# Attention and a two-layer MoE block on one core: batch 0 masked by a bias matmul, one casting DMA queue for the weights and batch 1, four second-layer tiles at once, PSUM banks assigned by hand

## The chip, the cores and the metric

The kernel runs on one core of a Trainium2 chip. The metric is the device time of the core in microseconds (us). Before the change it was 321.75 us, the median of three runs (321.38 to 325.4).

The engines are named as in the profile: PE is TensorE (PEld its weight loads), DVE is VectorE, ACT is ScalarE, POOL is GpSimd, SP is SyncE. The profiler also records the clock that the chip grants TensorE; in these traces it is either full (1.00) or half (0.50).

## The reference, cut to what matters

```python
def _attn_ref(q, k, v):            # (8, 8, 576, 64), float32
    scores = scale * np.matmul(q, k.transpose(0, 1, 3, 2))
    mask_local = (rel >= 0) & (rel < 32)                       # heads 0 to 3
    mask_strided = (rel >= 0) & (pos_k % 32 == pos_q % 32)     # heads 4 to 7
    attn = softmax(np.where(masks, scores, -1e9))
    return np.matmul(attn, v)

def _moe_ref(x, w_in, w_out):      # x: 4608 tokens x 512, hidden size 2048
    r = np.maximum(x @ w_in, 0.0)
    return (r * r) @ w_out
```

A *unit* is one pair of heads of one batch. Each batch has four: units 4b and 4b+1 are local, 4b+2 and 4b+3 strided. A *chunk* is 512 of the 4,608 tokens, and there are nine. A chunk's first layer is 16 ReLUs of 128x512; its second layer is four output tiles with four groups of four matmuls each. Batch 0's attention has to be done before chunk 0 can be, and batch 1's before chunk 1.

## The kernel before

The kernel fills PE with MoE matmuls and puts the attention of later batches, step by step, between the groups of four matmuls. The steps of a unit are T (transposes of q and k), S (scores, exponentials, mask), D (probabilities times v, then the division by the row sum on DVE) and E (the transposition of the result for the MoE). For batch 0 there is nothing to fill with, and it has its own order. The matmuls write into eight banks of the memory PSUM: five for attention (`pt`), two for the first layer (`ph`), one for the second (`py`).

```python
    ps_h = ctx.enter_context(tc.tile_pool(name="ps_h", bufs=2, space=PS))
    ps_y = ctx.enter_context(tc.tile_pool(name="ps_y", bufs=1, space=PS))
    ps_t = ctx.enter_context(tc.tile_pool(name="ps_t", bufs=5, space=PS))
    ...
    def step_S(u):                       # scores of one unit into four banks, then
        ...
        expo(0, 0)                       # the exponentials on ACT, one a tick,
        later(1, lambda: expo(0, 1), u)  # and the masks as products on DVE
        later(2, lambda: (masks(0), expo(1, 0)), u)
        later(3, lambda: expo(1, 1), u)
        later(4, lambda: masks(1), u)
    ...
        # end of batch 0's order: n = sums, o = products with v, part = the first three
        # ReLU rows of chunk 0, unit by unit as its rows of x come
        order = [...
                 (due(d), 0), (n(c), 0), (o(c), 0), (lambda: part((a, b), (0,)), 0), (n(d), 0), (o(d), 0),
                 (lambda: part((a, b), (1, 2)), 0), (lambda: part((c,)), 0), (lambda: part((d,)), 0)]
    ...
    def loads(b):                        # a batch's loads and casts; for b == 1 also the w_out blocks
        ...
        w_out(0)
        if b < XB:
            load_qk_str(u + 2)
        cast_qk_local(u, pool2)
        w_out(1)
        cast_qk_local(u + 1, pool2)
        ...
        w_out(2)
        cast_v_local(u)
        cast_v_local(u + 1)
        w_out(3)
    ...
    for part in range(4):                # chunk 0's second layer: three output tiles at once,
        for j, pool in ((0, ps_h), (1, ps_h), (2, None)):
            add(0, 2, 4 * j + part, pool)
    for part in range(4):                # then the fourth
        add(0, 2, 12 + part, ps_h)
```

The softmax here doesn't subtract the row's maximum and nothing guards it: scores larger than these inputs give would overflow.

Of the kernel before, what the change touches and what calls it, by code (L numbers as in the profile page):

```python
# [14 lines left out]
def kernel(  # L15
# [30 lines left out]
    x_pool = ctx.enter_context(tc.tile_pool(name="x_pool", bufs=2))  # L46
    g_pool = ctx.enter_context(tc.tile_pool(name="g_pool", bufs=2))
# [6 lines left out]
    ps_h = ctx.enter_context(tc.tile_pool(name="ps_h", bufs=2, space=PS))  # L54
    ps_y = ctx.enter_context(tc.tile_pool(name="ps_y", bufs=1, space=PS))
    ps_t = ctx.enter_context(tc.tile_pool(name="ps_t", bufs=5, space=PS))
# [16 lines left out]
    ones = singles.tile([128, D], BF16)  # L73
    b0 = g_pool.tile([128, 16, 512], BF16, name="g_sb").rearrange("p a c -> p (a c)")
# [4 lines left out]

    ph_n = [0]  # L80

    def ph_tile():
        ph_n[0] += 1
        return ps_h.tile([128, 512], FP32, name="ph")

    nc.scalar.preload_act_table_set("natural_log_exp_and_others")
# [12 lines left out]
    def load_qk_local(u, eng, gate=None):  # L99
        b, p = units[u]  # L100
        s = st.setdefault(u, {})
        for name, src in (("q", q), ("k", k)):
# [7 lines left out]
            if gate is not None and name == "q":  # L110
                nc.gpsimd.tensor_copy(t[0:1, 0, 0:1], gate)
            eng.dma_start(out=t, in_=src[b, 2 * p:2 * p + 2]
                          .rearrange("h (p j) d -> p h (j d)", j=6))
            s[name + "f"] = t
# [71 lines left out]

    def load_v_str(u, eng):
        b, p = units[u]
        t = v_st.tile([SP_, 2, NJ * D], FP32, name="v_st")
        eng.dma_start(out=t, in_=v[b, 2 * p:2 * p + 2]  # L190
                      .rearrange("h (p j) d -> p h (j d)", j=NJ))
        st.setdefault(u, {})["vf"] = t
# [32 lines left out]
    def step_T(u, name):  # L225
# [5 lines left out]
        pt = ps_t.tile([128, S], BF16, name="pt")  # L231
# [13 lines left out]
        if name == "q" and u not in (1, 2, 3):  # L245
            nc.scalar.copy(o, i)
        else:
            nc.vector.tensor_copy(o, i)
# [5 lines left out]
    def step_S(u):  # L254
# [8 lines left out]
        banks = [[None, None], [None, None]]  # L263
        for half in range(2):
            for row in range(2):
                banks[row][half] = ps_t.tile([128, 512], FP32, name="pt")
            for i in range(hn):
                t = half * hn + i
                klo = w * t
                for row in range(2):  # L270
# [4 lines left out]
                    else:  # L275
                        lhsT, rhs = kT[rows, klo:klo + kn], qT[rows, w * t:w * (t + 1)]
                    nc.tensor.matmul(banks[row][half][0:kn, w * i:w * (i + 1)], lhsT, rhs,  # L277
                                     start=True, stop=True)

        def expo(row, half):  # L280
            lo = S * row + S // 2 * half
            nc.scalar.activation(e[0:kn, lo:lo + S // 2], banks[row][half][0:kn, 0:S // 2],  # L282
                                 AF.Exp, scale=scale)

        def masks(row):
# [3 lines left out]
            if u < 2:  # L289
                nc.vector.memset(x[0:32, 0], 0.0)  # L290

        expo(0, 0)
# [5 lines left out]
    def load_v_first():  # L298
        src = v[0, 0:4].rearrange("h (t p) d -> p (h t) d", p=QL)
        dst = b0[:, 0:n_l].rearrange("p (n d) -> p n d", d=D)  # L300
        nc.gpsimd.dma_start(out=dst[32:128], in_=src)
        nc.gpsimd.dma_start(out=dst[0:32, 1:4 * NL], in_=src[64:96, 0:4 * NL - 1])
        nc.gpsimd.dma_start(
            out=b0[0:SP_, n_l:n_l + n_s].rearrange("p (h c) -> p h c", h=4),
            in_=v[0, 4:8].rearrange("h (p j) d -> p h (j d)", j=NJ))

    def step_N(u):
        e, local = st[u]["e"], is_local(u)
        kn, hw = (128 if local else SP_), S // 2
        for half in range(2):  # L310
            pn = ph_tile() if u in first_order[0:2] else ps_t.tile([128, 512], FP32, name="pt")
# [7 lines left out]
    def step_O(u):  # L319
# [3 lines left out]
        for half in range(2):  # L323
            po = ps_t.tile([128, 512], FP32, name="pt")
# [17 lines left out]
    def step_D(u, part):  # L342
# [14 lines left out]
        po = ps_t.tile([128, 6, D + 1], FP32, name="pt")  # L357
# [3 lines left out]
        if part == 0:  # L361
            s["x"] = x_pool.tile([w, tot, D], BF16, name="x_l" if is_local(u) else "x_s")
# [11 lines left out]
    def step_E(u):  # L374
# [11 lines left out]
        px = ps_t.tile([128, S], BF16, name="pt")  # L386
# [17 lines left out]
    def mm1(c, ff, kks=range(4), order=range(4), pool=None):  # L404
# [3 lines left out]
        if kks[0] == order[0]:  # L408
            phs[ff] = ph_tile() if pool is None else pool.tile([128, 512], FP32, name="py")
# [13 lines left out]
    def mm2(c, i, pool=None):  # L423
        j, part = divmod(i, 4)
        g = gs[c]
        if part == 0:
            ys[c, j] = ps_y.tile([128, 512], FP32, name="py") if pool is None else ph_tile()
# [4 lines left out]
        if part == 3:  # L432
            y = y_pool.tile([128, 512], FP32, name="y")
            nc.scalar.copy(y, py)  # L434
            r0 = 512 * c + 128 * j
# [7 lines left out]
    def warm(n):  # L443
        if n:
            pw = ps_y.tile([128, 512], FP32, name="py")
# [257 lines left out]
```

## Time and profile before

| stage of the kernel before | from, to (us) | length | what limits it |
|---|---|---|---|
| batch 0's attention | 0 to 24.5 | 24.5 | hand-overs PE, ACT, DVE; half clock from 12.9 to 23.1 |
| first layer of chunk 0 | 24.5 to 37.3 | 12.8 | PE |
| second layer of chunk 0, batch 1's attention in it | 37.3 to 62.6 | 25.3 | PE, with 4.2 us of short waits |
| chunks 1 to 8 | 62.6 to 319.6 | 257.0 | PE |

The prediction below shows the page's PE and clock lines, the stage table, the waits and some of the second-layer stage. One more view is needed to read the result: PE in order of time at the end of batch 0. The columns are start and length in us, engine, line, operation with its tiles, how many, and in brackets how long PE stood idle just before and for whom.

```profile
21.07 0.63 PE L412 MATMUL ph<-xt,w_in_b 128*128 128x512 bf16 x1 [0.33 <-DVE xt L335]
21.64 0.69 PE L314 MATMUL pt<-e,ones 128*64 128x288 bf16 x4
22.12 0.69 PE L332 MATMUL pt<-e,g_sb 128*64 128x96 bf16 x12
22.74 0.78 PE L412 MATMUL ph<-xt,w_in_b 128*128 128x512 bf16 x2
...
24.49 0.59 PE L412 MATMUL ph<-xt,w_in_b 128*128 128x512 bf16 x2
```

L332 is the products with v, L412 the first layer's pieces. The last product (22.12) comes before nearly all pieces, so DVE can divide its rows while PE works through the pieces of the other units. The last piece follows at 24.49 with hardly a wait.

### The profile page before, as it was taken

Reading aid. Unit: us, or ns where it says so; the run is one execution under the profiler, and the core shown is the slowest. Engines: PE = TensorE matmul, PEld = TensorE weight load, DVE = VectorE, ACT = ScalarE, POOL = GpSimd, SP = SyncE. Lnnn points to the kernel's source line nnn. Section 1 sums busy time; section 2 is a strip of 40 time slices with the busy share of each in tenths; the row PEclk is TensorE's granted clock in tenths of the full one; section 3 lists DMA queues with packets and bytes.
Section 4 is the critical chain, followed back from the end, with each engine's and each line's share of the span. In section 5 each row is a group of like instructions: output and inputs, shape, how many; then the busy total and the mean of one; then the engine's idle time right before and its main releaser. Section 6 shows DMA issues by size and latency. Waiting matters only on the chain.

```text
span 319.6 us, 6138 instructions
## 1 busy us (share of the span) xinstructions
PE 300.0 (94%) x2322; PEld 149.5 (47%) x2364; DVE 170.7 (53%) x414; ACT 163.7 (51%) x337; POOL 87.8 (27%) x114
## 2 busy tenths in 40 slices
PE   7789978898999989999999999999999999999995
PEld 3454545444555444444444444444444444444442
DVE  6476463677956975676585557555555222222200
ACT  4576644477655755554554455545543443434311
POOL 8605472473930713271182015000000000000000
PEclk9859999999999999999999999999999999999999
DMA  7999999999999999999797677000411110000021
GB/s 182 172 205 227 221 155 251 186 328 208 198 162 210 197 212 182 212 242 188 183 211 167 145 159 133 35 33 33 53 51 36 55 42 36 33 33 35 35 96 66
DMA packets 87220, 44.79 MB, mean 140 GB/s; under 512 B 71768, under 2 KB 80376, under 8 KB 87000
## 3 DMA queue, kind: packets, MB, share of 16 engines
q1 hardware_dynamic: 77448, 34.81, 53.3%
q0 software_dynamic: 9744, 9.60, 18.9%
q8 instruction: 18, 0.29, 0.4%
q14 instruction: 10, 0.08, 0.1%
HBM read 36.89 MB, written 12.98 MB: 156 GB/s over the span
## 4 chain that ended last, share of the span: by engine, by line
PE 78%; DMA 9%; DVE 6%; ACT 3%; issue 2%; POOL 1%; SPq 0%; ACTq 0%; POOLq 0%
PE ph L412 33%; PE py L430 26%; PE ph L430 10%; PE pt L359 3%; PE pt L277 3%; DMA w_out_b<-in_moe_w_out_dram 3%; DMA q_st<-in_q_dram 3%; DMA kT_s<-in_k_dram 3%; DVE xt L396 1%; PE pt L388 1%; DVE e L288 1%; PE pt L233 1%; DVE g_sb L419 1%; ACT r L418 1%; ACT e L282 1%
## 5 line engine op out<-in xcount | busy, mean ns | idle before, releaser
L412 PE MATMUL ph<-xt,w_in_b 128*128 128x512 bf16 x557 | 143.3, 380 | 3.3 <-DVE xt L396 1.9
L418 ACT ACTIVATE r<-ph 128x512 bf16<-128x512 f32 x143 | 85.3, 597 | 99.5 <-PE ph L412 96.2
L419 DVE TENSOR_TENSOR g_sb<-r 128x512 bf16<-128x512 bf16 x144 | 71.2, 496 | 102.4 <-ACT r L418 101.9
L430 PE MATMUL py<-w_out_b,g_sb 128*128 128x512 bf16 x383 | 100.2, 379 | 1.3 <-issue 0.5
L430 PEld LDWEIGHTS <-g_sb 128*128 128x128 bf16 x576 | 52.9, 98 | 60.8 <-issue 4.3
L412 PEld LDWEIGHTS <-w_in_b 128*128 128x128 bf16 x576 | 51.7, 98 | 54.5 <-issue 1.3
L282 ACT ACTIVATE e<-pt 128x288 bf16<-128x288 f32 (+1 forms) x128 | 48.8, 406 | 17.0 <-PE pt L277 16.9
L430 PE MATMUL ph<-w_out_b,g_sb 128*128 128x512 bf16 x166 | 40.7, 379 | 1.9 <-DMA w_out_b<-in_moe_w_out_dram 1.2
L181 POOL CAST vl<-vl_st 128x768 bf16<-128x768 f32 x14 | 12.4, 886 | 60.2 <-DMA vl_st<-in_v_dram 58.1
L359 PEld LDWEIGHTS <-e 128*128 128x128 bf16 (+1 forms) x392 | 21.0, 97 | 15.6 <-DVE e L288 0.5
L371 DVE TENSOR_TENSOR x_s<-pt,rinv 72x384 bf16<-72x384 f32 (+1 forms) x42 | 21.4, 509 | 1.4
L288 DVE TENSOR_TENSOR e<-e,mask_str 72x576 bf16<-72x576 bf16 x32 | 18.0, 563 | 5.9 <-ACT e L282 5.6
L122 POOL CAST q_l<-q_st 96x768 bf16<-96x768 f32 x15 | 13.0, 865 | 21.9 <-DMA q_st<-in_q_dram 19.4
L288 DVE TENSOR_TENSOR e<-e,mask_loc 128x576 bf16<-128x576 bf16 x32 | 16.7, 523 | 1.7 <-ACT e L282 1.7
L122 POOL CAST k_l<-k_st 96x768 bf16<-96x768 f32 x15 | 13.3, 885 | 13.9 <-DMA k_st<-in_k_dram 13.8
L370 DVE RECIPROCAL rinv<-pt 96x6 f32<-96x6 f32 (+2 forms) x70 | 12.9, 184 | 7.8 <-PE pt L359 7.8
L434 ACT COPY y<-py 128x512 f32<-128x512 f32 x25 | 14.7, 587 | 4.0 <-PE py L430 4.0
L371 DVE TENSOR_TENSOR x_l<-pt,rinv 96x384 bf16<-96x384 f32 x28 | 15.5, 553 | 1.8 <-DMA xt<-x_l 0.9
L434 ACT COPY y<-ph 128x512 f32<-128x512 f32 x11 | 6.4, 586 | 19.4 <-PE ph L430 19.4
L197 POOL CAST vs<-v_st 72x1024 bf16<-72x1024 f32 x14 | 15.4, 1126 | 1.6 <-DMA v_st<-in_v_dram 1.3
L359 PE MATMUL pt<-vs,e 72*128 72x65 bf16 x224 | 13.7, 193 | 0.1
L182 POOL CAST vl<-vl_st 32x640 bf16<-32x640 f32 x14 | 11.9, 850 | 0.9
(77 smaller groups left out, 154.2 us busy)
## 6 DMA issues: line engine op xcount, KB each, us to landing
out_dram<-y SPq DMA_DIRECT2D x36, 256.0 KB, 2.0
vl_st<-in_v_dram SPq DMA_DIRECT2D x28, 144.0 KB, 4.0
v_st<-in_v_dram SPq DMA_DIRECT2D x14, 288.0 KB
q_st<-in_q_dram SPq DMA_DIRECT2D x8, 288.0 KB, 7.1
k_st<-in_k_dram SPq DMA_DIRECT2D x8, 288.0 KB, 7.9
q_st<-in_q_dram SPq DMA_DIRECT2D x16, 144.0 KB, 3.8
k_st<-in_k_dram SPq DMA_DIRECT2D x16, 144.0 KB, 5.9
w_in_b<-in_moe_w_in_dram POOLq DMA_DIRECT2D x4, 512.0 KB, 9.4
```

The costliest lines, as they stand in the source:

```text
L122: copy(t.rearrange("p j h d -> p h j d"), s[name + "f"].rearrange("p h (j d) -> p h j d", j=6))
L197: (copy or nc.gpsimd.tensor_copy)(t[:, :, 0:D], s["vf"].rearrange("p h (j d) -> p (h j) d", d=D))
L282: nc.scalar.activation(e[0:kn, lo:lo + S // 2], banks[row][half][0:kn, 0:S // 2], AF.Exp, scale=scale)
L288: nc.vector.tensor_tensor(x, x, m.to_broadcast([kn, n, w]), op=ALU.mult)
L359: nc.tensor.matmul(po[:, n - n0, :], e[0:kn, pos(n):pos(n) + 128], rhs[0:kn, src(n), 0:D + 1], start=True, stop=True)
L370: nc.vector.reciprocal(rinv[0:w, 0:m], po[0:w, 0:m, D:D + 1])
L371: nc.vector.tensor_tensor(x, po[0:w, 0:m, 0:D], rinv[0:w, 0:m].to_broadcast([w, m, D]), op=ALU.mult)
L412: nc.tensor.matmul(ph, w_in_b[:, kk, 128 * ff:128 * (ff + 1)], xt[kk][:, 512 * c:512 * (c + 1)], start=(kk == order[0]), stop=(kk == order ...
L418: nc.scalar.activation(r, ph, AF.Relu)
L419: later(1, lambda: nc.vector.tensor_tensor(g[:, ff, :], r, r, op=ALU.mult))
L430: nc.tensor.matmul(py, g[:, ff, 128 * j:128 * (j + 1)], w_out_b[:, ff, :], start=(ff == 0), stop=(ff == 15))
L434: nc.scalar.copy(y, py)
```

## The change

There are three intents. (1) Batch 0's masks leave DVE: a matmul writes minus 30,000 times the forbidden places into the PSUM bank first, and the scores accumulate on it. More dummy matmuls ("fillers") are to keep the clock full, and one load of batch 0's v moves from GpSimd's queue to ScalarE's, a third queue beside GpSimd's and SyncE's. (2) The w_out blocks and the q, k and strided v rows of batch 1 go through one casting queue on GpSimd in the order in which they are needed. (3) Chunk 0's second layer works on all four output tiles at once, the fourth in a bank taken from attention, and batch 1's steps are placed by hand at given groups, most of them in one lump at group 24. Banks are no longer taken from pools but from lists in strict rotation. The diff also has smaller edits that the cut below leaves out: batch 0's transposes go to the first layer's banks, its unit 1 is cast on DVE instead of GpSimd, and the loads of later batches are issued at other groups. The diff, cut to its core:

```diff
+    banks = {nm: [psum.tile([128, 512], FP32, name=f"{nm}{i}") for i in range(n)]
+             for nm, n in (("ph", 2), ("py", 1), ("pt", 5))}
+    def bank(nm):
+        t = banks[nm].pop(0)
+        banks[nm].append(t)
+        while id(t) in unread:
+            run_due(lambda x: x[1] == unread[id(t)])
+        return t
 ...
+                pss[row][half] = bank("pt")
+                if u < 4:
+                    bias = ...
+                    nc.tensor.matmul(pss[row][half][0:kn, 0:S // 2], ident[0:kn, 0:kn], bias,
+                                     start=True, stop=False, skip_group_check=True)
 ...
+        # (step, fillers after it)
+        order = [(t(0, "q"), 2), (t(0, "k"), 3), (S_(0), 2), (cast1("q"), 0), (t(2, "q"), 1), (t(2, "k"), 2),
+                 (cast1("k"), 0), (S_(2), 1), (n(0), 1), (t(3, "q"), 1), (t(3, "k"), 1), (S_(3), 1), (n(2), 1),
+                 (t(1, "q"), 1), (t(1, "k"), 1), (o(2), 1), (S_(1), 1), (n(3), 1), (o(0), 1), (n(1), 1),
+                 (lambda: part((a, b)), 0), (o(3), 0), (lambda: part((c,)), 0), (o(1), 0),
+                 (lambda: part((d,)), 0)]
 ...
+    def loads_1():
+        load_w_out(0)
+        load_qk_local_sw(4); load_qk_str(6)                      # (lines joined here)
+        load_w_out(1)
+        load_qk_local_sw(5); load_qk_str(7); load_v_str_sw(6); load_v_str_sw(7)
+        load_w_out(2); load_w_out(3)
+        ...                                                      # v of units 4, 5 on SyncE; the casts
 ...
     for part in range(4):
-        for j, pool in ((0, ps_h), (1, ps_h), (2, None)):
+        for j, pool in ((0, "ph"), (1, "ph"), (2, None), (3, "pt")):
             add(0, 2, 4 * j + part, pool)
-    for part in range(4):
-        add(0, 2, 12 + part, ps_h)
 ...
+    second(20, T_(6, "q"), T_(6, "k"), S_(6), T_(4, "q"), T_(4, "k"))
+    second(21, S_(4), T_(5, "q"))
+    second(22, T_(5, "k"))
+    second(23, S_(5))
+    second(24, *D_all(4), T_(7, "q"), T_(7, "k"), E_(4), S_(7), *D_all(5), E_(5), *D_all(6))
+    second(25, E_(6))
+    second(26, *D_all(7))
+    second(27, E_(7))
```

## The prediction

> **What bounds the kernel now.** I read the page first, then a table by stage, then who PE waited for in the one stage that the change rebuilds, then that stage in order of time.
>
> ```profile
> PE 300.0 (94%) x2322; PEld 149.5 (47%) x2364; DVE 170.7 (53%) x414; ACT 163.7 (51%) x337; POOL 87.8 (27%) x114
> ...
> PEclk9859999999999999999999999999999999999999
> ```
>
> PE is busy 94% of the 319.6 us span, so the bound is TensorE and a change can win only PE's idle time or its slow clock. The clock line says where: slices 2 and 3 (8 to 24 us) ran at 0.8 and 0.5 of full speed, the rest at 1. The stage table shows where PE idles (columns: length of the stretch, busy us of PE, PEld, DVE, ACT, POOL, then clock, DMA share, GB/s):
>
> ```profile
> 24.40:37.30 12.90, 12.59 (x68) 5.89 (x68) 7.39 (x16) 9.33 (x17) 6.80 (x10) 1.00 1.15 225
> 37.30:62.30 25.00, 20.83 (x248) 12.05 (x251) 14.27 (x34) 11.88 (x27) 13.38 (x18) 1.00 1.13 207
> ...
> 119.50:151.70 32.20, 31.67 (x253) 15.68 (x257) 20.41 (x47) 16.81 (x36) 12.94 (x16) 1.00 1.19 206
> ```
>
> The stages are batch 0's attention (0 to 24.4), first layer of chunk 0 (to 37.3), second layer of chunk 0 with batch 1's attention between its tiles (to 62.3), then the rest. From 119.5 on PE idles only 0.5 us per 32 us: nothing to win. The change touches the first 62 us. There the second-layer stage idles 25.00 - 20.83 = 4.2 us, which these waits make up:
>
> ```profile
> PE ph L430 <- DMA w_out_b<-in_moe_w_out_dram: 1.2, 1, 1.2
> PE pt L277 <- DVE kT L248: 1.1, 2, 0.6
> PE pt L388 <- DVE x_s L371: 0.8, 2, 0.5
> PE pt L277 <- ACT e L282: 0.5, 1, 0.5
> ```
>
> One late weight block costs 1.2 us; the rest are short waits for DVE and ACT inside attention, short because a group of second-layer matmuls stands between nearly every two attention steps:
>
> ```profile
> 54.20 0.81 PE L430 MATMUL ph<-w_out_b,g_sb 128*128 128x512 bf16 x3 [0.16 <-issue]
> 54.85 0.42 PE L388 MATMUL pt<-ident,x_l 96*128 96x96 bf16 x6
> 55.10 1.03 PE L430 MATMUL py<-w_out_b,g_sb 128*128 128x512 bf16 x4
> 55.97 0.53 PE L359 MATMUL pt<-vs,e 72*128 72x65 bf16 x12
> 56.34 1.03 PE L430 MATMUL ph<-w_out_b,g_sb 128*128 128x512 bf16 x4
> ```
>
> **What the Trainium skill says.** "TensorE: Matmul & The Clock Gate", section "What's actually happening": the array runs at half clock after an idle window of about 3.4 us and at full clock after a busy one. The trace agrees in kind: PE is busy in 5.83 of the 8 us from 8 to 16, and the clock record halves from 12.9 to 23.1 us (10.24 us, three such windows). "DMA: Bandwidth & Descriptors", section "Issuing engines are not separate DMA queues": all queues share the same 16 engines. The trace agrees: with q and k on SyncE's queue and w_out on GpSimd's, packets of 1,024 B that had run at 200 per us alone fall to about 100. "PSUM — Partial Sum Buffer", section "The four PSUM rules": a matmul with the start flag clears the accumulate bits of its whole bank, so the bias matmul must carry the flag and the score matmuls must not. That is how the change writes it; no run yet shows it.
>
> **Part 1: batch 0 masks as a bias (0 to 24.4 us).** Removed from DVE: eight mask products of 0.45 us and four memsets of 0.10, 4.0 us. Added on PE: 16 bias matmuls of 288 columns (512 columns take 0.216 us, so 0.12 each, 1.9 us) and 14 more filler matmuls (22 instead of 8, 3.0 us). ACT's work stays. DVE's products are partly in the chain, but ACT becomes the next bound: from the scores of the second unit on it has three units of exponentials (4 x 0.33) and four normalizers (0.71 + 0.68), 3 x 1.32 + 4 x 1.39 = 9.5 us. In the trace ACT works from 12.25 to 23.58 there, 11.3 us, so 1.8 us at most comes free. Against it stands the DMA: the first masked unit waits for its k rows until 10.86 us, and now one v tile (1,152 packets of 256 B; 743 such packets fell in the us from 57 on, so 1.55 us) is fetched at the same time on a third queue. I take 0.7 us of delay. Batch 0 ends about 1.1 us earlier: last piece of the first chunk at 23.4 instead of 24.5.
>
> **Part 2: one casting queue.** Counted from packets: a w block of 512 packets takes 2.56 us at 200 per us; q and k of a local unit about 1.5, of a strided unit 1.44, v of both strided units 1.44. w_in lands at 26.0 before and, with the duplicate v load gone, about 25.7 after. Adding down the new queue: w_out block 0 at 28.3, q and k of units 4 and 6 at 31, block 1 at 33.7, units 5 and 7 at 36.5, and with 3.1 us of v tiles between them block 2 at 43.4 and block 3 at 46. Before, the last block was issued at 44.84 and took at least 6.2 us to land: 51.1. So the weights come 5 us sooner and the wait of 1.2 us goes. GpSimd's casts of q and k now stand behind the issue of block 3, which waits for block 1: units 4's are ready about 36.8 rather than 28.7. That is why the new order begins batch 1 only after the first four second-layer groups, where before three transposes (0.26 each) were done in the first layer.
>
> **Part 3: four tiles at once, batch 1 in a lump.** First layer: 13 groups of 4 x 0.216 and the leftover pieces, 12.1 us, from 23.4 to 35.5. Four groups on block 0: 3.45 us, to 38.9. From here (t = 0) I went down the new instruction order of PE, ACT and DVE by hand, each instruction starting when the one before it on its engine and its operands and bank were done, with durations of the trace before: transpose 0.26, scores 0.36 to 0.40, second-layer group 0.86, ACT copy 0.64, exponential 0.33, DVE copy 0.46 (strided units) or 0.75 (local), mask 0.45, reciprocal and product 0.73 for a local half, 1.9 for a strided unit. The fourth output tile holds one of the five attention banks, so scores (four banks) and transposes wait for each other's readers. Results: unit 6's scores wait 0.66 for the k copy; unit 4's k transpose waits 1.5 for the third exponential of unit 6; its scores 0.44; unit 5's transposes and scores 1.1; then in the lump with no second-layer group in it, unit 4's output transpose waits 1.9 for DVE (0.73 + two masks + 0.73), unit 7's scores and unit 5's products 0.9, unit 5's output transpose 1.9, the last two transposes 0.9 each. Sum 10.2, with small ones 10.9 us. PE's own work in the stage is 12 groups (10.4) and 6.3 of attention. So batch 1 takes 23.3 us up to its last transpose, and five groups (4.3 us) come after it: t = 27.6, the second chunk starts at 66.5.
>
> **The sum.** Before, the second chunk effectively starts at 62.6 (62.3 with one wait for a copy). After: 66.5, +3.9 us. From there PE's order is the same in both kernels, and it is PE-bound: unchanged. Median before 321.75 + 3.9 = 325.7 by this walk.
>
> **Rivals.** (a) The walk is too strict: every idle us of PE in it is a hand-over between ACT, DVE and PE, and an error of 0.1 us in each of some thirty hand-overs is 3 us. Then only the weights' 1.2 us and batch 0's 1.1 count, and the time is 318 to 320. For it: the steps are placed by hand at particular groups, which looks like tuning on measurements. Against it: DVE alone has 13 us of work in the stage, and before needed a group between each pair of steps to hide it. (b) The lump cools the clock: between t = 11 and 17.6 PE works about 1.3 of 6.6 us, less than in the stretch of batch 0 that lost the clock. Half clock for 7 to 10 us over eight groups costs 3 to 5 us more: 328 to 331. Against it: the windows may fall so that each holds enough. (c) The 14 extra fillers keep the clock full in batch 0, where before it was half for 10.24 us. PE is not the chain's main part there (ACT is), so this gives at most 1 to 1.5 us more: 324. (d) The v loads of units 4 and 5, now issued only after block 3's issue, come too late: due by unit 4's products at 49, expected landed and cast at 41 and 44. Eight us of slack, so unlikely.
>
> **Range and chances.** I weigh the walk (about 325.7) at one half, rival (a) at a third and (b) at a sixth, and shade the point to 323.3. PE's idle before 62 us leaves at most about 6 us to win even if all went well (4.2 in the second-layer stage, some 2 in batch 0), just under the 6.4 us that are 2%; so faster by over 2% has 4 in 100. Slower by over 2% (above 328.2) needs the clock loss as well: 11 in 100. Range 317.0 to 329.0.
>
> **What would show it.** Right: DVE has no mask products before 24 us; the last piece of batch 0 at 23 to 24 us; last w_out block landed by 47; no PE wait on w_out; PE idle of 9 to 12 us between 38 and 66, named by DVE x_l, x_s, kT and by ACT e; the first tile of the second chunk at 65 to 67. Wrong: a second chunk that starts before 62; PE idle under 6 us in that stage; a w_out wait still there; a half clock outside batch 0 (rival b); or a difference that appears after the second chunk starts, where I expect none.

## The result, and the profile after

The changed kernel took 335.49 us (median of four runs, 334.81 to 336.59) against 323.57 us for the kernel before in the same rounds (321.38 to 326.63). The ratio is 1.041, with a 95% interval of 1.035 to 1.047. Here and below, a ratio is the mean time of one kernel's runs over that of the other's runs of the same rounds, so it is not quite the ratio of the medians quoted. Executions over 1.5% slower than the fastest of the same kernel are left out of the means. The change is slower by 4%; the prediction was 323.3 us, with a range up to 329.0.

The page of the changed kernel has these two lines:

```profile
PE 310.7 (93%) x2395; PEld 151.8 (46%) x2395; DVE 170.5 (51%) x407; ACT 163.7 (49%) x337; POOL 93.4 (28%) x121
...
PEclk9999989699999999999999999999999999999999
```

The clock line has moved its dip. Batch 0 (slices 1 to 3) is at full clock now, and slices 6 and 8 (42 to 50 and 58 to 67 us), where the second layer of chunk 0 runs, are not. The clock record gives half clock from 46.8 to 50.2 and from 60.4 to 67.3 us, 10.24 us in all.

The table by stage has the same columns as in the prediction (length, busy us of the five engines, clock, DMA share, GB/s):

```profile
0.00:28.20 28.20, 23.23 (x243) 10.92 (x244) 14.53 (x49) 13.93 (x33) 17.17 (x30) 1.00 1.17 200
28.20:39.50 11.30, 11.28 (x53) 5.15 (x53) 6.97 (x15) 8.11 (x14) 6.54 (x10) 1.00 1.25 203
39.50:74.40 34.90, 25.89 (x262) 14.51 (x261) 15.11 (x34) 12.72 (x28) 18.08 (x23) 0.85 0.66 136
```

The last stage is the one that took 25.0 us before (37.3 to 62.3). It takes 34.9 us, of which PE idles 34.90 - 25.89 = 9.0 us. Before, it idled 4.2.

The time lost shows where the ReLUs and output copies on ACT start, before against after, in the two profiled runs:

| mark | before (us) | after (us) | difference |
|---|---|---|---|
| first ReLU (end of batch 0) | 24.91 | 27.57 | +2.7 |
| first ReLU of chunk 1 (second-layer stage done) | 63.60 | 75.42 | +11.8 |
| first ReLU of chunk 2 | 102.78 | 115.32 | +12.5 |
| last output copy | 315.96 | 328.79 | +12.8 |
| end of span | 319.6 | 333.1 | +13.5 |

Whom PE waited for in the second-layer stage (us in total, times, longest):

```profile
PE pt L437 <- DVE x_l L420: 4.4, 2, 2.2
PE pt L256 <- ACT e L315: 2.4, 4, 1.3
PE pt L437 <- DVE x_s L420: 0.6, 2, 0.3
PE pt L305 <- DVE kT L271: 0.6, 1, 0.6
```

L437 is the transposition of an attention result (E), which waits for DVE's division. L256 is a transposition of q or k, which waits until an exponential has read the bank that it is to get. No wait on w_out is left: its blocks landed at 27.7, 33.8, 40.3 and 43.7 us, where before they landed at 33.1, 39.4, 48.2 and 51.1. In order of time, PE alone:

```profile
46.69 0.60 PE L256 MATMUL pt<-ident,k_l 96*128 96x96 bf16 x6 [1.33 <-ACT e L315]
47.09 1.91 PE L482 MATMUL ph<-w_out_b,g_sb 128*128 128x512 bf16 x4
...
54.50 0.53 PE L407 MATMUL pt<-vl,e 128*128 128x65 bf16 x12
54.87 0.42 PE L256 MATMUL pt<-ident,qT_s 72*128 72x72 bf16 x8
55.13 0.43 PE L256 MATMUL pt<-ident,kT_s 72*128 72x72 bf16 x8
57.76 0.43 PE L437 MATMUL pt<-ident,x_l 96*128 96x96 bf16 x6 [2.20 <-DVE x_l L420]
...
62.52 0.66 PE L437 MATMUL pt<-ident,x_l 96*128 96x96 bf16 x6 [2.19 <-DVE x_l L420]
62.98 1.08 PE L407 MATMUL pt<-vs,e 72*128 72x65 bf16 x16
63.88 1.90 PE L482 MATMUL ph<-w_out_b,g_sb 128*128 128x512 bf16 x4
```

In the lump (54.5 to 63.9) no second-layer group (L482) stands between the attention steps, so PE waits out DVE's two masks and two divisions in full, 2.20 and 2.19 us. And the groups at 47.09 and 63.88 took 1.91 and 1.90 us, where one at full clock takes 1.03: they lie in the half-clock stretches.

The end of batch 0, to set beside the view shown before:

```profile
21.84 0.39 PE L501 MATMUL py<-xt 128*128 128x512 bf16 x1
22.06 1.03 PE L461 MATMUL ph<-xt,w_in_b 128*128 128x512 bf16 x4
22.93 0.59 PE L461 MATMUL py<-xt,w_in_b 128*128 128x512 bf16 x2
23.45 0.45 PE L380 MATMUL pt<-e,g_sb 72*64 72x72 bf16 x16
25.12 0.59 PE L461 MATMUL ph<-xt,w_in_b 128*128 128x512 bf16 x2 [1.22 <-DVE xt L383]
...
25.86 0.45 PE L380 MATMUL pt<-e,g_sb 128*64 128x96 bf16 x12
27.16 0.59 PE L461 MATMUL ph<-xt,w_in_b 128*128 128x512 bf16 x2 [0.86 <-DVE xt L389]
```

L380 is the products with v, L461 the first layer's pieces, L501 a filler. Two of the products now stand *after* the pieces of the first two units, and then each piece waits for DVE to divide the rows that were just made (1.22 and 0.86 us). The last piece comes at 27.16 us instead of 24.49.

### The profile page after: what moved, and what is told of

Read it like the earlier page. It is cut to its first block, busy times and chain, and to the rows that moved or that the text cites.

```text
span 333.1 us, 6234 instructions
## 1 busy us (share of the span) xinstructions
PE 310.7 (93%) x2395; PEld 151.8 (46%) x2395; DVE 170.5 (51%) x407; ACT 163.7 (49%) x337; POOL 93.4 (28%) x121
## 3 DMA queue, kind: packets, MB, share of 16 engines
q0 software_dynamic: 9088, 10.24, 18.4%
## 4 chain that ended last, share of the span: by engine, by line
PE 86%; DVE 6%; ACT 3%; DMA 3%; issue 1%; POOL 0%; DVEq 0%; ACTq 0%; POOLq 0%
PE ph L461 37%; PE py L482 26%; PE ph L482 10%; PE pt L407 3%; PE pt L305 3%; DMA kT_s<-in_k_dram 3%; PE pt L437 1%; DVE e L321 1%; PE pt L256 1%; ACT e L315 1%; PE py L501 1%; DVE xt L445 1%; PE pt L482 1%; DVE x_l L420 1%; DVE x_s L420 1%
## 5 line engine op out<-in xcount | busy, mean ns | idle before, releaser
L461 PE MATMUL ph<-xt,w_in_b 128*128 128x512 bf16 x572 | 144.1, 379 | 4.3 <-DVE xt L445 2.0
L482 PE MATMUL py<-w_out_b,g_sb 128*128 128x512 bf16 x400 | 102.7, 379 | 0.0
L482 PEld LDWEIGHTS <-g_sb 128*128 128x128 bf16 x576 | 53.8, 99 | 62.6 <-issue 5.0
L461 PEld LDWEIGHTS <-w_in_b 128*128 128x128 bf16 x576 | 51.9, 98 | 56.3 <-issue 2.6
L482 PE MATMUL ph<-w_out_b,g_sb 128*128 128x512 bf16 x160 | 40.4, 396 | 0.0
L419 DVE RECIPROCAL rinv<-pt 96x6 f32<-96x6 f32 (+2 forms) x70 | 12.9, 184 | 11.8 <-PE pt L407 8.5
L137 POOL CAST q_l<-q_st 96x768 bf16<-96x768 f32 x12 | 10.9, 909 | 28.3 <-DMA q_st<-in_q_dram 28.3
L321 DVE TENSOR_TENSOR e<-e,mask_loc 128x576 bf16<-128x576 bf16 x28 | 14.5, 522 | 2.5 <-ACT e L315 2.5
L407 PE MATMUL pt<-vs,e 72*128 72x65 bf16 x224 | 13.5, 197 | 1.1 <-ACT e L315 1.1
L137 POOL CAST k_l<-k_st 96x768 bf16<-96x768 f32 x12 | 11.0, 915 | 12.0 <-DMA k_st<-in_k_dram 11.8
L220 POOL CAST vs<-v_st 72x1024 bf16<-72x1024 f32 x12 | 13.5, 1148 | 0.9 <-DMA v_st<-in_v_dram 0.6
L501 PE MATMUL py<-xt 128*128 128x512 bf16 x31 | 11.8, 452 | 1.3 <-DVE xt L616 1.3
## 6 DMA issues: line engine op xcount, KB each, us to landing
w_in_b<-in_moe_w_in_dram POOLq DMA_DIRECT2D x4, 512.0 KB, 11.5
```

What stands on the lines that cost most here:

```text
L137: copy(t.rearrange("p j h d -> p h j d"), s[name + "f"].rearrange("p h (j d) -> p h j d", j=6))
L220: (copy or nc.gpsimd.tensor_copy)(t[:, :, 0:D], s["vf"].rearrange("p h (j d) -> p (h j) d", d=D))
L321: nc.vector.tensor_tensor(x, x, m.to_broadcast([kn, n, w]), op=ALU.mult)
L407: nc.tensor.matmul(po[:, n - n0, :], e[0:kn, pos(n):pos(n) + 128], rhs[0:kn, src(n), 0:D + 1], start=True, stop=True)
L461: nc.tensor.matmul(ph, w_in_b[:, kk, 128 * ff:128 * (ff + 1)], xt[kk][:, 512 * c:512 * (c + 1)], start=(kk == order[0]), stop=(kk == order ...
L482: nc.tensor.matmul(py, g[:, ff, 128 * j:128 * (j + 1)], w_out_b[:, ff, :], start=(ff == 0), stop=(ff == 15))
```

## The experiments

My theory after reading the traces had four parts. The lump without groups in it costs most. Half clock is a part of that. The bank that the fourth output tile holds is another. In batch 0, fillers and the late products stand in PE's chain. The rivals are those of the prediction, and each run below names its own. Fifteen kernels were run, and all gave correct results. Times are medians of all runs, and the second time of a pair is that of the kernel before in the same rounds. The marks (first ReLU and so on) are from the one profiled run of each kernel.

### The lump: spread it, free the bank, fill it

**e1_spread**: the changed kernel with batch 1's steps spread over groups 16 to 32, at most three to a group.

```diff
-    second(20, T_(6, "q"), T_(6, "k"), S_(6), T_(4, "q"), T_(4, "k"))
-    ... (the lump)
+    second(16, T_(6, "q"), T_(6, "k"))
+    second(17, S_(6))
+    second(18, T_(4, "q"))
+    ...
+    second(23, S_(7), D_(4, 1))
+    second(24, T_(5, "q"), E_(4))
+    ...
+    second(31, E_(5))
+    second(32, E_(7))
```

> The changed kernel with only the order of batch 1's steps changed: the same steps spread over second-layer groups 16 to 32, at most one or two between groups, the late-loaded unit 5 last. Theory (the lump costs): PE's idle time from the start of the second layer to the second chunk falls from about 11 us to 3 to 5 us, the clock stays full there, and the time falls by 8 to 10 us, to about 326. Rival (late data): v of unit 4 lands at 44.4 us and the casts of q and k of unit 5 stand behind it, so the waits only move to GpSimd's casts, and the time falls by less than 4 us.

It took 328.02 us against 325.19, ratio 1.013 (0.998 to 1.028). The four runs differ widely (324.51 to 332.74), and so do their mean clocks (1.000 to 0.974). The profiled one is slow, with half clock from 12.9 to 30.0 us, so only the part after that is read. From the first ReLU to that of chunk 1 it took 38.45 us, against 47.85 in the changed kernel and 38.70 in the kernel before. The clock was full there. The waits for DVE's x_l are gone from the list:

```profile
PE pt L407 <- DVE e L321: 1.3, 1, 1.3
PE pt L437 <- ACT y L486: 0.7, 1, 0.7
```

Two runs confirm the size: e6_spread_nofill (spread) needs 39.24 us for this stretch and e2_nofill (lump, the same batch 0) 49.29. With the fourth tile in an attention bank, the lump and all that follows from it cost about 10 us.

**e8_three**: the changed kernel, lump and all, but three output tiles at once and the fourth after them, so that attention keeps five banks.

```diff
-        for j, pool in ((0, "ph"), (1, "ph"), (2, None), (3, "pt")):
+        for j, pool in ((0, "ph"), (1, "ph"), (2, None)):
             add(0, 2, 4 * j + part, pool)
+    for part in range(4):
+        add(0, 2, 12 + part, "ph")
```

> The changed kernel with three output tiles of chunk 0 at once and the fourth after them, as before, so that attention has all five banks; the lump as changed. Theory (the fourth tile's bank makes transposes wait for exponentials, 2.4 us in the profile): these waits fall to under 1 us and the time by 1 to 2 us. Rival (the lump is bound by the VectorE and ScalarE chain, a fifth bank only moves the wait): less than 0.7 us.

It took 330.46 us against 322.62, ratio 1.027 (1.019 to 1.035). From the first ReLU to that of chunk 1 it took 42.19 us instead of 47.85: 5.7 us for one bank. The waits on ACT's exponential at L256 are gone, and those on x_l are halved:

```profile
PE pt L437 <- DVE x_l L420: 2.1, 2, 1.2
```

Half clock lasted 6.8 us (56.2 to 63.0) instead of 10.2, so part of the 5.7 us is clock. Freeing the bank, with the clock that goes with it, takes away more than half of the 10 us.

**e12_order_three**: three output tiles instead of four, with the steps spread (the other run of this pair is e7_order, told below). The edit is that of e8_three.

> The run with batch 1 spread, no extra fillers and two products moved forward, plus three output tiles at once rather than four, so that attention keeps five banks. Theory: with the steps spread a group stands between them and the bank is hardly waited for: within 1 us of the four-tile run of the same form (324.4 us, ratio 1.008), against 5.7 us in the lump. Rival: the fourth tile's bank also costs in the spread form, 3 us or more: ratio below 1.000.

It took 324.20 us against 322.56, ratio 1.004 (0.996 to 1.011). The four-tile version, e7_order, took 324.38 us. The two are within 1 us, as the theory said, although they were not run in the same rounds; their ratio intervals overlap. In the two profiled runs the stretch from the first ReLU to that of chunk 1 even took longer with three tiles, 42.24 us against 40.28. So no cost of the bank is shown without the lump. The likely reason, which no run tests, is that with a group between each pair of steps a bank has mostly been read by the time it is needed again. The reverse holds too: with five banks the stretch took no longer in the lump (e8_three, 42.19 us) than spread (e12_order_three, 42.24). That comparison is not a clean one, as batch 0 ends 4.0 us sooner in e12_order_three and PE then waits 2.2 us for GpSimd's casts of v, a wait that e8_three does not have. So the 10 us belong to the lump and the missing bank together; what the lump costs with all five banks stays open.

**e5_fill** and **e9_fill2**: fillers in the lump's longest waits, 6 + 9 + 9 in the first and 9 + 9 in the second. The 6 stand before the k transposition of unit 4, in group 20; the cut shows the others.

```diff
-    second(24, *D_all(4), T_(7, "q"), T_(7, "k"), E_(4), S_(7), *D_all(5), E_(5), *D_all(6))
+    second(24, *D_all(4), T_(7, "q"), T_(7, "k"), fill(9), E_(4), S_(7), *D_all(5), fill(9), E_(5), *D_all(6))
```

> The changed kernel with 24 filler matmuls added in PE's three longest waits of the second-layer stage (6 ahead of unit 4's k transpose, 9 ahead of the output transposes of units 4 and 5), written into the attention bank that the next transpose overwrites. The waits stay. Theory (half clock costs 3 to 4 us there): the clock record shows no half clock between 40 and 75 us and the time falls by 3 to 4 us. Rival (PE's clock does not matter in a chain of DVE and ACT): the time changes by less than 1 us or rises by the fillers that outlast their wait.

> The changed kernel with only the two sets of 9 fillers ahead of the output transposes of units 4 and 5; the earlier set of 6, which itself waited for its bank and then cost 2.4 us, is left out. Theory: the second stretch of half clock (60 to 67 us) does not come and the second chunk starts 2 to 3 us earlier, so the time falls by 2 to 3 us. Rival: the clock falls there anyway, or DVE sets the pace and the time stays within 1 us.

e5_fill took 335.07 us against 325.19, ratio 1.037 (1.023 to 1.050). Half clock shrank from 10.2 to 3.4 us, and the stretch from the k transposition of unit 4 to the last step of batch 1 from 23.27 to 20.67 us. But the first six fillers had to wait for a bank themselves, and the chain up to that k transposition grew from 3.80 to 6.25 us:

```profile
47.37 0.53 PE L733 MATMUL pt<-w_in_b 128*128 128x512 bf16 x1 [1.33 <-ACT e L315]
48.12 1.91 PE L733 MATMUL pt<-w_in_b 128*128 128x512 bf16 x4 [0.22 <-issue]
49.82 0.69 PE L256 MATMUL pt<-ident,k_l 96*128 96x96 bf16 x6
```

L733 is the fillers. In the changed kernel the transposition itself took that wait of 1.33 us; here the fillers take it and then stand before the transposition, at half clock too. e9_fill2, without those six, took 334.30 us against 322.62, ratio 1.039 (1.033 to 1.046). Its half clock moved to 48.6 to 55.4 us and lasted 6.8 us, now over second-layer groups. Neither gains. What e5_fill shows is the size of the clock's part: 2.6 us over the same steps when all but the first 1.1 us of the stretch runs at full clock. The same follows from the changed kernel's own records: the nine sets of matmuls and transposes that lie in its half-clock stretches took 3.8 us longer in sum than sets of the same form and number at full clock. About 3 us is thus half clock, in agreement with rival (b) of the prediction.

### Batch 0: fillers, bias, the order of the products

**e2_nofill**: the changed kernel with 13 of the 23 fillers in batch 0's order taken out, which leaves the 10 before the scores of unit 2. (The texts say 12 of 22; I had miscounted by one, so the change adds 15 and not 14.)

> The changed kernel without the fillers from the scores of unit 2 on (12 of 22 taken away). Theory (fillers stand in PE's chain of batch 0): batch 0 ends 2.0 to 2.8 us earlier (12 fillers of 0.22 us less what ACT then makes PE wait), and the time falls by about 2 us. Rival (the fillers hold the clock up): the clock halves between 12 and 24 us as in the kernel before, batch 0 ends no earlier or later, and the time is the same within 1 us or worse.

It took 334.30 us against 325.19, ratio 1.035 (1.025 to 1.046). The first ReLU came at 25.63 us instead of 27.57, and the clock stayed full through all of batch 0 without those fillers. A part of such a difference is chance, as the early part of batch 0 varies from run to run: its first normalizer on ACT (the logarithm and exponential that turn a sum into its inverse) ended between 14.4 and 15.9 us in the 17 traces. From that end to the first ReLU the changed kernel takes 12.80 us (12.80 to 12.84 in six traces of the same batch 0 with at most 0.3 us of half clock there), and e2_nofill 10.73. So 13 fillers cost 2.1 us, 0.16 each, and bought nothing in this run. The gain did not show in the total: the lump behind had half clock for 13.7 us instead of 10.2 and took 1.4 us longer.

**e3_nobias**: the changed kernel with the masks as products on DVE again.

```diff
-                if u < 4:
+                if False:                       # no bias matmul
 ...
-                                     start=u > 3, stop=True, skip_group_check=u < 4)
+                                     start=True, stop=True)
 ...
+                masks(row)                      # after the two exponentials of each row
```

> The changed kernel with batch 0 masked on VectorE after the exponential, as before, and no bias matmuls; all else as changed. Theory (the 16 bias matmuls stand in PE's chain, 0.25 to 0.37 us a pair, about 2.4 us): batch 0 ends 1.5 to 2.5 us earlier. Rival (the bias pays, because the mask products of 0.45 us stood between the exponential and the sums): batch 0 ends later by up to 2 us.

It took 337.64 us against 325.19, ratio 1.047 (1.037 to 1.057), but this run doesn't settle the question: batch 0 ran at half clock from 13.6 to 27.2 us, and the first ReLU came at 32.44. The comparison is one of clocks, not of masks.

**e6_spread_nofill** and **e7_order** go step by step from e1_spread. The first takes the 13 fillers out. The second also moves the two late products in front of the pieces:

```diff
-                 (t(1, "q"), 0), (t(1, "k"), 0), (o(2), 0), (S_(1), 0), (n(3), 0), (o(0), 0), (n(1), 0),
-                 (lambda: part((a, b)), 0), (o(3), 0), (lambda: part((c,)), 0), (o(1), 0),
+                 (t(1, "q"), 0), (t(1, "k"), 0), (o(2), 0), (S_(1), 0), (n(3), 0), (o(0), 0), (o(3), 0), (n(1), 0),
+                 (lambda: part((a, b)), 0), (o(1), 0), (lambda: part((c,)), 0),
```

> The changed kernel with batch 1's steps spread and without the 12 later fillers, both edits seen alone before. If the two costs stand in different stages and add (9.4 us and 1.9 us), the time is 2 us above the kernel before or less (ratio 1.000 to 1.008), with the first relu at 25.6 us and the second chunk's at 64 to 65. Rival (the fillers did hold the clock in batch 0, where the spread run lost it even with them): the clock halves between 12 and 24 us in this profile and the first relu comes after 27 us.

> As the run before it, and the last two weighted sums of batch 0 (units 3 and 1) moved ahead of the first-layer pieces that had stood between them, so that VectorE's products run beside PE. Theory (in the changed order these products are waited for twice, 1.2 and 0.9 us, with PE idle): the first relu comes 2 to 3 us earlier than in that run (22.6 to 23.6) and the time is 1 to 2 us below the kernel before. Rival (ACT's normalizers end last there whatever the order): less than 0.7 us.

e6_spread_nofill took 325.35 us against 322.62, ratio 1.009 (1.001 to 1.018), with the first ReLU at 26.22 us. e7_order took 324.38 us, ratio 1.008 (1.003 to 1.013), with the first ReLU at 23.20 us, 1.7 us before that of the kernel before. Its end of batch 0:

```profile
20.96 0.59 PE L461 MATMUL py<-xt,w_in_b 128*128 128x512 bf16 x2
21.48 0.45 PE L380 MATMUL pt<-e,g_sb 128*64 128x96 bf16 x12
21.86 0.60 PE L461 MATMUL ph<-xt,w_in_b 128*128 128x512 bf16 x2
```

The waits of 1.22 and 0.86 us in front of the pieces are gone. The two first ReLUs are 3.0 us apart, but a part of that is the early part of batch 0, and e6_spread_nofill had half clock in the last 0.4 us before its first ReLU. Counted from the end of the first normalizer, e7_order takes 8.75 us (e12_order_three, with the same batch 0, 8.76), and e2_nofill, with the old order, no extra fillers and full clock, 10.73. The order of two products is thus worth 2.0 us. The medians gained only 1 us of this. Two things stand against it: in the second-layer stage of e7_order PE waits 1.6 us for GpSimd's casts of v, a wait that e6_spread_nofill does not have, and the mean clock was 0.992 in the profiled run of e7_order and 0.979 in its other three.

**e10_order_nobias**: e7_order with DVE's masks instead of the bias, by the edit of e3_nobias.

> The run with batch 1 spread, no extra fillers and two products moved forward, but with batch 0's masks as products on VectorE again, no bias matmuls. The bias alone, with the same products' order and no fillers on either side. If the bias is worth what the prediction gave it (ACT takes over as the bound, 1.1 us gained in all), the first ReLU comes at 24.3 to 25 us against 23.2 with the bias, 0.3 to 0.6% slower in all. Rival: PE's 1.9 us of bias matmuls cost as much as VectorE's 4.0 us of products, first ReLU within 0.5 us of 23.2. Comparable only if the clock's half stretches in batch 0 are alike.

It took 324.36 us against 322.56, ratio 1.004 (0.997 to 1.011), which is the same time as e7_order. Its batch 0 had half clock for 13.7 us (11.5 to 25.2), and the first ReLU came at 27.52 us, so the batch 0 of the two can't be compared at one clock. In the total the bias gains nothing measurable; the mean clocks are alike there (0.977 to 0.979, against 0.979 in three of the four runs of e7_order). Whether it helps by keeping the clock is only suggested: of the profiled runs, the three without bias matmuls (the kernel before, e3 and e10) had 10 to 14 us of half clock in batch 0, and of the fourteen with them, eleven had at most 0.8 us before the first ReLU, two had 6.8 and one 17.1.

### The first part alone, and the 1 us that comes later

**e14_part1**: only the change's batch 0. Loads, order and output tiles of the rest are as in the kernel before, and the order of PE's instructions after batch 0 is the same.

```diff
-    loads_1()
+    loads(1)                                   # with the w_out blocks in it, as before
-    second(20, ...) to second(27, ...)
+    plan(2, 8, 0, 0)                           # batch 1's steps by weight, as before
-        for j, pool in ((0, "ph"), (1, "ph"), (2, None), (3, "pt")):
+        for j, pool in ((0, "ph"), (1, "ph"), (2, None)):
```

> Only the change's batch 0 (bias matmuls, 22 fillers, products in the change's order, v loads on three queues); from the end of batch 0 on everything, loads and order of batch 1 included, as in the kernel before. My theory: the first ReLU comes 2.7 us later than before if the clock stays full in batch 0 (as in the changed kernel), nothing else changes: ratio about 1.008, 324 to 326 us, and the 1 us that appeared in the second and third chunk of the changed kernel is absent, as it comes from the new places of the loads of batches 2 and 3. Rival: the prediction's Part 1, batch 0 ends 1.1 us earlier, ratio 0.996. If the 1 us appears here too, its cause is not the loads but the banks or the order within attention.

It took 325.33 us against 322.56, ratio 1.007 (0.999 to 1.015). The first ReLU came at 28.43 us, 3.5 us later than before (the last 0.8 us of it at half clock), so in batch 0 Part 1 alone is a loss. In the total this run does not show it, as its interval includes 1; e15_part1_banks below, with the same batch 0, does (1.005 to 1.013). And the later 1 us appears here too (between ReLU 24 and ReLU 32, counted from 0: 29.91 us against 28.78), so it comes neither from the new loads nor from the lump. All 16 traces other than that of the kernel before have it (29.84 to 30.70 us), with bias matmuls and without; of the kernel before there is one trace. In this stretch the trace shows:

```profile
87.94 0.83 POOL L137 CAST k_l<-k_st 96x768 bf16<-96x768 f32 x1
87.99 1.87 DVE L321 TENSOR_TENSOR e<-e,mask_str 72x576 bf16<-72x576 bf16 x1
...
88.71 0.83 POOL L137 CAST q_l<-q_st 96x768 bf16<-96x768 f32 x1
...
90.47 0.74 DVE L271 COPY kTl<-pt 128x576 bf16<-128x576 bf16 x1
90.52 0.41 ACT L315 ACTIVATE e<-pt 72x288 bf16<-72x288 f32 x1
90.98 0.28 PE L407 MATMUL pt<-vs,e 72*128 72x65 bf16 x4 [0.98 <-ACT e L315]
```

There are two suspects. The four products at 90.98 get, by strict rotation, the bank of the unit's last scores, whose exponential at 90.52 stands on ACT behind an output copy. In the kernel before, where the pool chose the bank, the same products (at 85.95 us) did not wait. The other suspect is DVE's mask product, 1.87 us beside two GpSimd casts where one alone takes 0.45 us, which delays the k copy at 90.47.

**e15_part1_banks**: e14_part1 with banks handed out by release, as the pool does.

```diff
     def bank(nm):
-        t = banks[nm].pop(0)
-        banks[nm].append(t)
+        l = banks[nm]
+        t = next((x for x in l if id(x) not in unread), l[0])
+        to_end(l, t)
 ...
             del unread[id(pss[row][half])]
+            to_end(banks["pt"], pss[row][half])
```

> The run with only the change's batch 0, but the five attention banks are handed out by release (the bank whose last reader came first in program order), as the pool of the kernel before does, instead of in strict rotation. In strict rotation the last four products of a strided unit get the bank of its last scores, whose exponential stands on ScalarE behind a copy of an output tile; by release they get a bank freed earlier. Theory: the 1.1 us that appears between ReLU 24 and ReLU 32 is gone (within 0.3 us), the rest as in the run before: ratio about 1.004. Rival: the 1 us comes from VectorE's mask product of 1.87 us beside GpSimd's casts, and stays.

It took 324.63 us against 322.03, ratio 1.009 (1.005 to 1.013). The wait of 0.98 us is gone, but the stretch took 30.06 us, no less: waits of 0.7 us (scores, for a k copy) and 0.5 us (scores, for a bank that DVE was reading) came in its place. My theory for the 1 us falls as stated. The rival isn't proved either, as in this run the product beside the casts at the same place took 1.09 us and not 1.87. The cause of this 1 us stays open.

**e17_after_banks**: the changed kernel with banks by release, by the same edit.

> The changed kernel with one thing different: attention banks handed out by release instead of in strict rotation. Theory: the second and third chunk lose their 1.1 us, and in the lump, with four banks left, some of the waits of PE for the exponential's bank go too: 331 to 334.5 us, ratio 1.026 to 1.037. Rival: strict rotation is what makes the lump slow, then 328 us or less.

It took 338.57 us against 322.03, ratio 1.050 (1.046 to 1.055), outside what both theories expected. Half clock lasted 3.4 us in the first layer and 17.1 us in the second-layer stage. The rival (that strict rotation makes the lump slow) falls, and so does my 331 to 334.5 us. In the lump, banks by release don't help.

### A version that beats both?

**e11_early**: e12_order_three with the v rows of units 4 and 5 loaded before the last two w_out blocks, the casts of q and k set around the last block, and batch 1's steps spread from group 12 on, as the kernel before has them. (The text says that the casts of v come before these blocks too; in the edit they stand behind both.)

```diff
     def loads_1():
         ...
-        load_v_str_sw(7)
-        load_w_out(2)
-        load_w_out(3)
         ...                                    # v of units 4, 5 on SyncE
+        load_v_str_sw(7)
+        load_w_out(2)
         cast_qk_local(4, pool2)
+        load_w_out(3)
+        cast_qk_local(5, pool2)
         cast_v_local(4)
-        cast_qk_local(5, pool2)
         cast_v_local(5)
 ...
-    second(16, T_(6, "q"), T_(6, "k"))
+    second(12, T_(6, "q"))
+    second(13, T_(6, "k"))
+    second(14, S_(6))
+    ...
```

> An attempt at a version that beats both: batch 0 with bias, no extra fillers and the products moved forward; three output tiles at once; batch 1's v loads and casts before the last two w_out blocks; batch 1's steps spread from group 12 on, in the first layer too, as before. Theory: batch 0 gains 1.7 us against before, the second-layer stage loses its 1.2 us wait on w_out, nothing else changes: 318 to 320 us, ratio 0.990 to 0.995. Rival: the v tiles in front delay w_out blocks 2 and 3 again and a wait on w_out of 1 us or more returns, or casts on GpSimd come late for the early steps: ratio 1.000 or more.

**e16_early_banks**: the same with banks by release.

> The best run so far (batch 0 with bias and without extra fillers, three output tiles, v tiles early, batch 1 spread) with the banks handed out by release. Theory: its 1.1 us between ReLU 24 and 32 goes too: 320.4 us, ratio 0.992. Rival: no change, 321.5 us, ratio 0.995.

e11_early took 321.47 us against 322.56, ratio 0.995 (0.987 to 1.004). From the first ReLU to that of chunk 1 it took 36.13 us, 2.6 us less than the kernel before, although batch 0 had 6.8 us of half clock in the profiled run. It is some 14 us below the changed kernel's time (in other rounds), but against the kernel before the interval includes 1: no difference is shown. e16_early_banks took 322.03 us against 322.03, ratio 1.001 (0.997 to 1.006); banks by release bring nothing here either.

## Why the prediction was wrong, point by point

Two steps failed. Part 1 had batch 0 end 1.1 us earlier, and it ended 2.7 us later. And the half clock in the lump, rival (b), was given a sixth of the weight instead of a place in the sum; it cost 2.6 to 3.8 us.

In its own terms, the walk gave the kernel +3.9 us. The profiled spans differ by 13.5 us. The 9.6 us between them are:

| term | the walk | measured | missed by |
|---|---|---|---|
| last piece of batch 0 | 23.4 | 27.2 | 3.8 |
| first layer of chunk 0 | 12.1 | 12.3 | 0.2 |
| second-layer stage | 31.0 (35.5 to 66.5) | 34.9 (39.5 to 74.4) | 3.9 |
| chunks 1 to 8 | unchanged | +1.0 | 1.0 |
| after the last output copy | unchanged | +0.7 | 0.7 |

**Part 1 failed**, at the sentence "Batch 0 ends about 1.1 us earlier". It ended 2.7 us later, 3.8 us off. The step took ACT as the next bound and set PE's 1.9 us of bias matmuls and 3.0 us of fillers aside as work beside it. The trace has PE busy nearly without a gap from 13 to 23.8 us, so PE is the chain there and each filler is in it: 13 of them cost 2.1 us (e2_nofill). And the step read the removed and added instructions but not the order of what stayed. Two products with v had moved behind the first-layer pieces, which costs 2.0 us (e7_order against e2_nofill). The two together, 4.1 us, account for the 3.8. With both put right, the first ReLU comes 1.7 us earlier than before (e7_order; 1.1 in e12_order_three), so the predicted gain was there in the idea and lost in the fillers and the order. The delay of 0.7 us by the DMA was not seen: the k rows landed at 10.69 us, before the change at 10.86.

**Rival (c)** was right in kind: the clock stayed full in batch 0 of the changed kernel. But the fillers are not shown to be the reason. Of the eight profiled runs with bias matmuls and all fillers, seven kept it (at most 0.8 us of half clock) and e1_spread lost it for 17.1 us; of the six without the 13 fillers, four kept it (at most 0.4 us) and e11_early and e16_early_banks lost it for 6.8 us.

**Part 2 held.** The prediction had the blocks at 28.3, 33.7, 43.4 and 46; they came at 27.7, 33.8, 40.3 and 43.7 us. The wait on w_out is gone, and rival (d) did not come about as a wait of PE: the casts of v, which it had at 41 and 44 us, were made at 44 to 50, before the products that need them at 54.5. It did come about in e7_order and e12_order_three, where batch 0 ends some 4 us sooner: PE waits 1.6 and 2.2 us for these casts.

**Part 3's walk had the waits right and left out its own rival.** PE idled 9.0 us in the stage for 10.9 predicted, so rival (a), a walk too strict, was worth 1.9 us by this count. The waits are the named ones: the two waits for x_l were put at 1.9 each and measured 2.2, the one for the third exponential at 1.5 and measured 1.3. PE's own work, though, fills 25.9 us of the records where the walk had 20.1 (16 groups, 13.8, and 6.3 of attention). What the walk lacked is the clock. Rival (b), that the lump cools the clock and costs 3 to 5 us more, is what came: 2.6 us by e5_fill, 3.8 by the records. (The other 2.0 us of these 5.8 may be the records' modelled ends, which cover idle time; no run shows it.) The step that failed is the weight of a sixth given to it, and before that the third given to rival (a), which drew the point from 325.7 down to 323.3. The walk's own numbers spoke against that: they had PE at work in 1.3 of 6.6 us of the lump, far less than in the 8 us where the kernel before had lost its clock. The rival should have been added to the sum, not weighed beside it; with it the walk gives 328.7 to 330.7.

**"Unchanged" from chunk 1 on** was wrong by 1.0 us, and by 0.7 us at the end. PE's order is indeed the same there. A kernel with the same loads and order as before and only the new batch 0 loses the first of the two also (e14_part1). Both stay unexplained. The second goes with the new loads and order of batch 1: from the start of the last output copy to the end the 14 traces that have them take 4.2 to 4.3 us, and the three that don't (the kernel before, e14_part1, e15_part1_banks) 3.5 to 3.6.

**What the table of idle time hid.** The fourth output tile's bank alone was worth 5.7 us in the lump (e8_three). The prediction named it as the cause of the waits but did not work out the same walk with five banks, which might have shown how much of the lump's cost was a choice of banks.

## What to carry to other kernels

When a change adds work to an engine that is already the chain, or moves steps past each other, walk the whole new order, also for what the diff does not add or remove; fillers that stand in the chain are not free (2.1 us for 13 here). Don't put dependent steps of one attention batch in a lump without matmuls between them, and don't take a PSUM bank from it at the same time: the waits add up, and then the clock falls too. Add the clock to the sum as a term as soon as a stretch of 3.4 us has PE at work for half or less of it: here all 15 such stretches were followed by half clock.

## What the Trainium skill lacked or had wrong

- "TensorE: Matmul & The Clock Gate", section "Why this matters for your kernels", advises to leave no PE idle gap over about 3 us. In these runs the clock halved with much shorter gaps: in the 3.41 us before 46.8 us of the changed kernel the longest was 1.33 us, and in those before 12.9 us of the kernel before 1.05 us, with PE busy 60% of them. (So the trace does not agree with the page's idle window even "in kind", as the prediction had it.) What told the two apart was the share of work. I cut the first 80 us of the 17 traces (the two kernels and the fifteen experiments) into windows of 3.41 us counted from a clock change, and summed PE's records in each. Of the windows at full clock, all 15 with PE busy for half or less were followed by half clock, 5 of 13 with 51 to 60%, none of 29 with 61 to 70%, and 2 of 277 above that. Elsewhere the page tells of a clock that swings when PE idles briefly and often, but it has no such share.
- The same page, section "What's actually happening", has full clock return after one busy window. Here 19 windows at half clock in which PE's records fill 70% or more were followed by another at half; e1_spread stayed at half for 17.1 us (five windows) in batch 0, the first four of them with PE 94 to 100% busy by its records. Why is open: a busy share by the profile's records, whose ends are modelled, need not be what the clock follows. The page warns that the clock has been seen stuck, and gives no condition.
- "SBUF — State Buffer", section "SBUF: two separate sides", says that whichever of DVE and GpSimd starts first holds their shared port pair for its whole instruction, where the DVE one has two SBUF inputs, as the mask product has, and the GpSimd one reads SBUF. The runs agree, and give the price that the page lacks. In the 17 traces a mask product alone took 0.45 us (median of 599). The 291 that began while a cast or copy of GpSimd ran took 0.73 us in the median and up to 2.19; of the 86 that began before it, 84 took less than 0.6.
- No page gives a price for one bank less for attention's hand-overs: in the lump it was 5.7 us (e8_three), and with a matmul group between the steps nothing measurable (e12_order_three).
